# GpSimd fills a scratch tile behind each of its indirect transfers, from item 4 of the expert stage on as well

## The chip, the cores and the metric

The kernel runs on one core of a Trainium2 chip. The metric is the device time of one execution in microseconds (us); the time of a kernel is the median of its timed runs.

## The reference

Channel attention over four batches, and then a two-level mixture of experts over all 14592 tokens (four groups of four experts, so 16 experts; each token goes to one). Everything is float32.

```python
# attention: q, k, v are (4, 3648, 256)
qn = q / (np.linalg.norm(q, axis=1, keepdims=True) + 1e-06)
kn = k / (np.linalg.norm(k, axis=1, keepdims=True) + 1e-06)
a = softmax(kn.transpose(0, 2, 1) @ qn / tau)      # 256 x 256 for each batch
x = (v @ a).reshape(14592, 256)
# experts: one group g, then one expert e of that group for each token
h = np.maximum(x[tokens] @ w1[g, e], 0.0)          # w1[g, e]: 256 x 1024
out[tokens] = (g_w * e_w)[:, None] * (h @ w2[g, e])  # w2[g, e]: 1024 x 256
```

## The kernel before

The first third of the run is attention: it makes the rows x of all tokens and the expert of each token, and GpSimd writes each row by an indirect transfer (a scatter, line 444) into a DRAM array `x_sorted`, in which every expert has slots of its own. Behind each scatter GpSimd runs `pause()` (line 158), a memset of 128x256 float32 in the tile `zero`. That tile is read once, by the indirect transfer of `zero_rows` (line 561), which lies in the stage of items 0 to 3.

The rest is the expert stage. It works through 28 items of 512 tokens of one expert. For each item there are eight steps (f = 0 to 7) of 128 hidden columns: `ffn1` makes `hmm` in PSUM (line 899), ScalarE makes its rounded part `hh` (line 908) and VectorE the remainder `hl` (line 909), and two steps later `ffn2` adds `hh` and `hl` times the second weights into `wacc` (lines 919 and 920). When an item is done, `finish` scales its four tiles of 128 tokens into `ys` (lines 936 and 937), and `send` writes each by an indirect transfer of GpSimd to `out` (line 948). Items 0 to 3 read their rows from `x_sorted` by ordinary transfers of the SP queue; for items 4 to 27 `fetch_x` gathers them by one indirect transfer of GpSimd into `xg` (line 510, in `gather`), two items ahead. SP then copies `xg` in 16 pieces into `xq` (line 687, in `quads_of`), and VectorE turns `xq` into `xT` (line 735, in `turn_x`).

Beside items 4 to 27 run six quads: a quad holds 32 tokens each of four experts, worked on side by side. Their rows come by `q_rows` (a gather, line 510 too), their results go out by `q_put` (line 1042). A last part, for what is left in blocks of 128 tokens (`s_rows`, `s_put`), runs only as often as the data needs; its lines do not occur in this trace, apart from the memsets that set up its tiles.

GpSimd and SP run their instructions in the order in which the program writes them, in the expert stage the other engines too. In item i, GpSimd's order is: the four sends of item i-1 (behind step f = 1), the gather of item i+2 and, in every fourth item, the gather of the next quad (f = 3), and `q_put` (f = 3 of a quad's fourth item). SP's order is: half of the quad weights (f = 3), the first weights of item i+2 (f = 5, line 662), the other half (f = 6), the 16 pieces of item i+2 (f = 7), and then the second weights of the next item (f = 1). ScalarE and VectorE split the weights `wraw` into `ww` (lines 709 and 710). In step f = 4 of the last item GpSimd drains its queue and all engines read the number of remaining blocks (lines 1200 and 1201).

Before the change `pause()` stands behind every scatter, behind the gathers of items 4 and 5 (`if i < 2`: i counts from item 4 there) and behind the sends of items 0 to 3 (`KPRE` is 4). It does not stand behind the later gathers and sends, nor behind `q_rows` and `q_put`.

Of the kernel before, what the change touches and what calls it, by code (L numbers as in the profile page):

```python
# [37 lines left out]
KPRE = 4  # L38
# [22 lines left out]
def attention_moe(ctx: ExitStack, tc, q, k, v, tau, w_group, w_expert, w1, w2, out):  # L61
# [21 lines left out]
    def ring(*shape, name):  # L83
        return rp.tile([P, *shape], F32, tag="ring", name=name, bufs=RING)
# [71 lines left out]
    def pause():  # L156

        POOL.memset(zero[:, 0:256], 0.0)
# [349 lines left out]
    def gather(rows, ix, per):  # L508
        src = xs_d.rearrange("(n t) w -> n (t w)", t=per)
        POOL.indirect_dma_start(out=rows.bitcast(I32), out_offset=None, in_=src,  # L510
                                in_offset=bass.IndirectOffsetOnAxis(ap=ix, axis=0),
                                bounds_check=NSLOT // per - 1, oob_is_err=False)
# [138 lines left out]
    def raw_tile():  # L651
        return wp.tile([P, 2048], F32, tag="wraw", name="wraw", bufs=3)
# [11 lines left out]
    def fetch_x(d, tb, i):  # L664

        if d is items[0]:
            d["xg"] = raw_tile()[:, 0:4 * RW].rearrange("p (t w) -> p t w", t=4)
        else:
            d["xg"] = ring(4, RW, name="xg")
        d["nv"] = tb[1][:, i:i + 1]  # L670
        if tb is not tb_pre:
            gather(d["xg"].rearrange("p t w -> p (t w)"), tb[2][:, i:i + 1], 4)
            if i < 2:
                pause()
            return
        s = SP.value_load(tb[0][0:1, i, 1:2], min_val=0, max_val=DUMMY)
        ins = SP.dma_start(d["xg"].bitcast(I32), xs_d[ds(s, BIG), :].rearrange("(p t) w -> p t w", t=4))
        early.append(ins.ins)
        for o in late:
            tc.declare_no_dep(ins.ins, o, reason="the first items' slots have been filled")  # L680
# [78 lines left out]
    items = [dict() for _ in range(NBIG)]  # L759
# [73 lines left out]
    xsp = lambda i: (lambda: split_x(items[i]))  # L833
    fw = lambda i, which: (lambda: fetch_w(*where(i), which))
    fx = lambda i: (lambda: fetch_x(*where(i)))

    def where(i):
# [16 lines left out]
    for t in range(TM, len(xs_at)):  # L854
# [18 lines left out]
        if k == 8:  # L873
            fetch_w(items[0], tb_pre, 0, "w1")
            fetch_x(items[0], tb_pre, 0)
            fetch_w(items[0], tb_pre, 0, "w2")
# [3 lines left out]
        if x == UX - 1:  # L880
            fetch_x(items[1], tb_pre, 1)
            fetch_w(items[1], tb_pre, 1, "w1")
            split_x(items[0])
# [47 lines left out]
    def put(d, t, src, on):  # L931
        ys = d["ys"]
        wcol = d["wc"][:, t:t + 1]
        if len(d["acc"]) == 4:
            a = d["acc"][t]
            ACT.activation(ys[:, t, :], a[:, 1, :], AF.Copy, scale=wcol)
            DVE.scalar_tensor_tensor(ys[:, t, :], a[:, 0, :], wcol, ys[:, t, :], ALU.mult, ALU.add)  # L937
        elif on == 0:
            ACT.activation(ys[:, t, :], src, AF.Copy, scale=wcol)
        else:  # L940
            DVE.tensor_scalar(ys[:, t, :], src, wcol, None, ALU.mult)
        if any(d is o for o in items[0:2]):
            held.append((d, t))
        else:
            send(d, t)

    def send(d, t):
        ins = POOL.indirect_dma_start(  # L948
            out=out, out_offset=bass.IndirectOffsetOnAxis(ap=d["ids"][:, t:t + 1], axis=0),
            in_=d["ys"][:, t, :], in_offset=None, bounds_check=N - 1, oob_is_err=False)  # L950
        for o in yscat:
            tc.declare_no_dep(ins.ins, o, reason="every token is in one slot")
        yscat.append(ins.ins)
        if any(d is o for o in items[0:KPRE]):
            pause()

    held = []

    def send_late(i):
        return lambda: [send(d, t) for d, t in held if d is items[i]]  # L960
# [24 lines left out]

    def q_rows(q):
        gather(qs["xg"][q % 2], tb_pc[2][:, q:q + 1], 1)

    def q_weights(q, st, half):

        t = raw_tile() if half == 0 else None
        for k in range(2):
            p = 2 * half + k
            e = SP.value_load(tb_pc[0][0:1, 4 * q + p, 0:1], min_val=0, max_val=E - 1)
            w = t[:, k * 1024:(k + 1) * 1024] if half == 0 else rp.tile([P, 1024], F32, tag="L", name="qw", bufs=2)
            if st < 2:
                SP.dma_start(w.rearrange("p (c f) -> p c f", c=2),
                             w1e[ds(e, 1), :, st * 512:(st + 1) * 512].rearrange("o (c p) f -> p (o c) f", p=P))
            else:
                SP.dma_start(w.rearrange("p (c f) -> p c f", c=4),  # L1000
                             w2e[ds(e, 1), (st - 2) * 512:(st - 1) * 512, :].rearrange("o (c p) f -> p (o c) f", p=P))
            qs["w", p] = w
# [36 lines left out]
    def q_put(q):  # L1039
        ids = qs["ids"][q % 2]  # L1040
        DVE.tensor_scalar(qs["y"], qs["a"][:, 0:C], qs["xg"][q % 2][:, C + 1:C + 2], None, ALU.mult)
        ins = POOL.indirect_dma_start(
            out=out, out_offset=bass.IndirectOffsetOnAxis(ap=ids, axis=0),
            in_=qs["y"], in_offset=None, bounds_check=N - 1, oob_is_err=False)
        for o in yscat:
            tc.declare_no_dep(ins.ins, o, reason="every token is in one slot")
        yscat.append(ins.ins)


    raws, pb = {}, {}  # L1050
# [123 lines left out]
    for n in range(len(seq) + lag):  # L1174
# [3 lines left out]
        if n < len(seq):  # L1178
            i, f = seq[n]
            j, jn = host(i), host(i + 1)  # L1180
            if f == 3:
                if KPRE < i + 2 < NBIG:
                    fetch_x(*where(i + 2))
                if jn is not None:
                    if jn % 4 == 0:
                        q_rows(jn // 4)
                    q_weights(jn // 4, jn % 4, 0)
# [37 lines left out]
        if lag <= n < len(seq):  # L1225
            i, f = seq[n - lag]
# [4 lines left out]
        if n == len(seq) + lag - 1:  # L1231

            d = items[NBIG - 1]
            d["ys"] = ring(4, C, name="ys")
            for t in (0, 2, 1, 3):
                tsl, a, wcol = slice(t * P, (t + 1) * P), d["acc"][t], d["wc"][:, t:t + 1]
                for f in range(8 - TAIL, 8):
                    PE.matmul(a, d["h", f][0][:, tsl], d["w2w"][:, :, f, :], start=False, stop=(f == 7), skip_group_check=True)
                ACT.activation(d["ys"][:, t, :], a[:, 1, :], AF.Copy, scale=wcol)
                for f in range(8 - TAIL, 8):  # L1240
                    PE.matmul(a[:, 0, :], d["h", f][1][:, tsl], d["w2h"][:, f, :], start=False, stop=(f == 7), skip_group_check=True)
                DVE.scalar_tensor_tensor(d["ys"][:, t, :], a[:, 0, :], wcol, d["ys"][:, t, :], ALU.mult, ALU.add)
                send(d, t)
# [93 lines left out]
```

## Time and profile before

| | us |
|---|---|
| median of 3 runs (lowest to highest) | 950.46 (949.25 to 953.48) |
| the profiled execution, its own time | 950.95 |
| its span, first to last instruction | 949.1 |
| TensorE busy, matmuls | 923.4 |
| VectorE busy | 698.3 |
| ScalarE busy | 480.5 |
| GpSimd busy | 338.0 |

The profile is of one execution. PE is TensorE's matmuls, PEld its weight loads, DVE VectorE, ACT ScalarE, POOL GpSimd, SPq the queue of SP. In a list of instructions a row gives the start and the length in us, the engine, the line, the operation, the tile written and the tiles read, and in brackets how long the engine stood idle before it and what ended that. In a list of waits a row gives the waiting engine and line, what it waited for, the total, the number of times and the longest.

### The profile page before, as it was taken

How to read it: one execution, taken by the hardware profiler on the slowest of the kernel's cores; microseconds unless marked ns; L12 is line 12 of the kernel's file. 1: busy time of each engine (PE TensorE's matmuls, PEld its weight loads, DVE VectorE, ACT ScalarE, POOL GpSimd, SP SyncE). 2: the span in 40 equal slices, each digit the busy share in tenths (PEclk: the TensorE clock that was granted, in tenths of full speed). 3: DMA queues.
4: the chain of work that ended last, by engine and by line, in shares of the span. 5: the costliest groups of instructions: out<-in, count | busy, mean ns of one | idle time of the engine just before them, and what ended most of it. 6: DMA issues, size and time to landing. Idle time of an engine off the chain costs nothing.

```text
span 949.1 us, 16996 instructions
## 1 busy us (share of the span) xinstructions
PE 923.4 (97%) x5620; PEld 768.9 (81%) x5620; DVE 698.3 (74%) x1478; ACT 480.5 (51%) x791; POOL 338.0 (36%) x443
## 2 busy tenths in 40 slices
PE   8999999997999999999999999999999999999996
PEld 7899998987899988777877887877777887787784
DVE  6889888666889886867875687567775967577752
ACT  6787777565654544444444444444444444344431
POOL 0002998876588662222211222222222222222112
PEclk9999999999999999999999999999999999999999
DMA  9975868364755677677677767777776667766630
GB/s 305 356 262 200 308 225 280 113 227 156 252 178 178 189 260 241 218 235 244 221 230 227 251 243 241 242 251 245 244 242 225 237 221 233 224 232 219 216 118 27
DMA packets 159171, 213.96 MB, mean 225 GB/s; under 512 B 63107, under 2 KB 117643, under 8 KB 159072
## 3 DMA queue, kind: packets, MB, share of 16 engines
q1 hardware_dynamic: 144128, 168.23, 54.4%
q0 software_dynamic: 14944, 44.54, 12.5%
q8 instruction: 46, 0.75, 0.3%
q14 instruction: 53, 0.43, 0.2%
HBM read 170.33 MB, written 31.39 MB: 213 GB/s over the span
## 4 chain that ended last, share of the span: by engine, by line
PE 47%; issue 21%; DVE 10%; DMA 8%; POOL 4%; ACT 4%; SPq 3%; another core or an unknown queue 2%; POOLq 0%; DVEq 0%; ACTq 0%
PE hmm L899 16%; PE xmm L332 8%; PE wacc L919 7%; PE yacc L928 5%; PE wacc L920 4%; PE sacc L227 3%; DMA wraw<-in_moe_w 3%; DVE qhT L1007 2%; DMA qkraw<-in_k 2%; DMA qw<-in_moe_w 2%; POOL out L948 2%; PE vtr L312 2%; DVE ww L710 2%; DVE hl L909 1%
## 5 line engine op out<-in xcount | busy, mean ns | idle before, releaser
L899 PE MATMUL hmm<-xth,ww 128*128 128x512 f32 x896 | 316.6, 394 | 1.6 <-issue 1.5
L908 ACT ACTIVATE hh<-hmm 128x512 fp32r<-128x512 f32 x222 | 131.1, 598 | 311.6 <-PE hmm L899 249.4
L919 PE MATMUL wacc<-ww,hh 128*128 128x512 f32 x752 | 275.9, 398 | 0.4 <-issue 0.4
L909 DVE SCALAR_TENSOR_TENSOR hl<-hmm,hh 128x512 fp32r<-128x512 f32 x222 | 150.7, 686 | 161.4 <-ACT hh L908 151.5
L948 POOL DMA_INDIRECT out<-ys,ids x112 | 111.0, 991 | 436.9 <-DVE ys L937 394.8
L920 PE MATMUL wacc<-ww,hl 128*128 128x256 f32 x752 | 213.6, 284 | 2.7 <-issue 1.3
L899 PEld LDWEIGHTS hmm<-xth,ww 128*128 128x128 f32 x896 | 168.0, 188 | 39.8 <-issue 1.7
L899 PE MATMUL hmm<-xtl,ww 128*128 128x512 f32 x448 | 177.4, 396 | 0.2 <-DVE xtl L750 0.2
L919 PEld LDWEIGHTS wacc<-ww,hh 128*128 128x128 f32 x752 | 141.3, 188 | 41.6 <-issue 5.8
L444 POOL DMA_INDIRECT x_sorted<-xs,si x112 | 134.5, 1201 | 67.6 <-issue 34.6
L920 PEld LDWEIGHTS wacc<-ww,hl 128*128 128x128 f32 x752 | 141.1, 188 | 20.0 <-DVE hl L909 10.7
L710 DVE TENSOR_TENSOR ww<-wraw,ww 128x1024 fp32r<-128x1024 f32 x112 | 136.4, 1218 | 6.8 <-ACT ww L709 5.3
L709 ACT ACTIVATE ww<-wraw 128x1024 fp32r<-128x1024 f32 x112 | 118.3, 1057 | 0.0
L899 PEld LDWEIGHTS hmm<-xtl,ww 128*128 128x128 f32 x448 | 84.4, 188 | 11.8 <-issue 1.2
L227 PE MATMUL sacc<-qkraw 128*128 128x256 f32 (+1 forms) x360 | 86.9, 384 | 1.0 <-DMA qkraw<-in_k 1.0
L332 PE MATMUL xmm<-ahi,vth 128*128 128x276 f32 (+1 forms) x232 | 70.0, 304 | 6.5 <-issue 4.0
L227 PEld LDWEIGHTS sacc<-qkraw 128*128 128x128 f32 (+1 forms) x360 | 65.3, 192 | 9.8 <-issue 1.5
L332 PE MATMUL xmm<-alo,vth 128*128 128x276 f32 (+1 forms) x232 | 67.5, 292 | 0.4 <-DVE alo L292 0.4
L332 PE MATMUL xmm<-ahi,vtl 128*128 128x276 f32 (+1 forms) x232 | 66.9, 289 | 0.0
L211 DVE TENSOR_TENSOR sqa<-sqa,sq 128x2048 f32<-128x2048 f32 (+1 forms) x28 | 57.5, 2055 | 9.6 <-ACT sq L203 8.1
L335 ACT ACTIVATE xs<-xmm 128x276 f32<-128x276 f32 x112 | 43.4, 404 | 38.7 <-PE xmm L332 25.1
L1007 DVE STREAM_TRANSPOSE qhT<-qh 32x128 f32<-32x128 f32 x192 | 57.6, 300 | 2.7
(269 smaller groups left out, 1269.5 us busy)
## 6 DMA issues: line engine op xcount, KB each, us to landing
wraw<-in_moe_w SPq DMA_DIRECT2D x55, 1024.0 KB
wraw<-in_moe_w SPq DMA_DIRECT2D x50, 512.0 KB
qw<-in_moe_w SPq DMA_DIRECT2D x48, 512.0 KB
vr<-in_v SPq DMA_DIRECT2D x28, 512.0 KB
qkraw<-in_q SPq DMA_DIRECT2D x26, 512.0 KB
qkraw<-in_k SPq DMA_DIRECT2D x26, 512.0 KB
xq<-xg SPq DMA_DIRECT2D x368, 32.0 KB
x_sorted<-xs,si POOLq DMA_INDIRECT x112
```

What stands on the lines that cost most here:

```text
L227: PE.matmul(d["acc"][:, c, :], kt[:rows, 1, cs], qt[:rows, 0, :], start=d.pop("first", True) and c == 0, stop=(g == NG), skip_group_check= ...
L332: PE.matmul(mm[:rows, :NE], vt[:, c, j * P:j * P + rows], at[:, c, :], start=(n == 0), stop=(n == 5))
L444: ins = POOL.indirect_dma_start(out=xs_d, out_offset=bass.IndirectOffsetOnAxis(ap=si[:rows, j:j + 1], axis=0), in_=xs[:rows, t, 0:RW].bitc ...
L709: ACT.activation(whs[n][:, s], raw[:, s], AF.Copy)
L710: DVE.tensor_tensor(wls[n][:, s], raw[:, s], whs[n][:, s], ALU.subtract)
L899: PE.matmul(mm, wt[:, c, fs], xt[:, c, :], start=(n == 0), stop=(n == 5))
L908: ACT.activation(hh, mm, AF.Relu)
L909: d["hl"] = DVE.scalar_tensor_tensor(hl, mm, 0.0, hh, ALU.max, ALU.subtract)
L919: PE.matmul(d["acc"][t], hh[:, tsl], d["w2w"][:, :, f, :], start=(f == 0), stop=(f == 7), skip_group_check=True)
L920: PE.matmul(d["acc"][t][:, 0, :], hl[:, tsl], d["w2h"][:, f, :], start=False, stop=(f == 7), skip_group_check=True)
L948: ins = POOL.indirect_dma_start(out=out, out_offset=bass.IndirectOffsetOnAxis(ap=d["ids"][:, t:t + 1], axis=0), in_=d["ys"][:, t, :], in_o ...
L1007: DVE.transpose(dst[a * PC:(a + 1) * PC, :, p * PC:(p + 1) * PC], src[p * PC:(p + 1) * PC])
```

## The change

Three conditions fall away or are added: `pause()` now follows the gather of every item from 4 on, every send, every quad gather and every quad write. The gathers and writes of the remaining blocks (`s_rows`, `s_put`) get none.

```diff
@@ fetch_x
             gather(d["xg"].rearrange("p t w -> p (t w)"), tb[2][:, i:i + 1], 4)
-            if i < 2:
-                pause()
+            pause()
             return
@@ send
         yscat.append(ins.ins)
-        if any(d is o for o in items[0:KPRE]):
-            pause()
+        pause()
@@ q_rows
     def q_rows(q):
         gather(qs["xg"][q % 2], tb_pc[2][:, q:q + 1], 1)
+        pause()
@@ q_put
         yscat.append(ins.ins)
+        pause()
```

`pause` itself is unchanged:

```python
    def pause():
        POOL.memset(zero[:, 0:256], 0.0)
```

## Rows read from the trace of the kernel before

**Rows 1.** The page's first part: busy us, share of the span, instructions of each engine
```profile
PE 923.4 (97%) x5620; PEld 768.9 (81%) x5620; DVE 698.3 (74%) x1478; ACT 480.5 (51%) x791; POOL 338.0 (36%) x443
```

**Rows 2.** Waits of PE from 352 us on, all of them: total, times, longest
```profile
PE wacc L1241 <- ACT ys L1239: 2.3, 4, 0.6
PE hmm L899 <- issue: 1.5, 4, 0.6
PE wacc L920 <- issue: 1.3, 3, 0.8
PE wacc L919 <- issue: 0.4, 1, 0.4
PE wacc L920 <- DVE hl L909: 0.2, 1, 0.2
```

**Rows 3.** Waits of the weight loads (PEld) from 352 us on, two of them
```profile
PEld wacc L920 <- DVE hl L909: 10.7, 24, 0.7
...
PEld qacc L1035 <- DMA xq<-xg: 0.7, 2, 0.4
```

**Rows 4.** Groups of POOL's instructions: busy us, mean ns, idle before
```profile
L158 POOL MEMSET zero<- 128x256 f32 x134 | 44.7, 334 | 0.1
```

**Rows 5.** POOL's instructions in order of time where sends are paused
```profile
347.46 0.33 POOL L158 MEMSET zero<- 128x256 f32 x1
347.95 0.97 POOL L948 DMA_INDIRECT out<-ys,ids  x1 [0.16 <-issue]
348.92 0.33 POOL L158 MEMSET zero<- 128x256 f32 x1
349.42 0.97 POOL L948 DMA_INDIRECT out<-ys,ids  x1 [0.16 <-issue]
```

**Rows 6.** POOL's instructions in order of time in a later item, without pauses
```profile
645.78 1.00 POOL L948 DMA_INDIRECT out<-ys,ids  x1 [13.21 <-DVE ys L937]
647.08 0.97 POOL L948 DMA_INDIRECT out<-ys,ids  x1 [0.30 <-issue]
...
650.92 1.05 POOL L510 DMA_INDIRECT xg<-x_sorted,ix_big  x1 [0.30 <-issue]
```

**Rows 7.** Waits of SP's queue between 400 and 900 us, the longest
```profile
SPq L687 <- DMA xg<-x_sorted,ix_big: 40.0, 16, 5.8
```

**Rows 8.** SP's queue in order of time, the same item
```profile
657.97 11.83 SPq L687 DMA_DIRECT2D xq<-xg  x16
670.65 0.41 SPq L662 DMA_DIRECT2D wraw<-in_moe_w  x1
674.26 2.17 SPq L1000 DMA_DIRECT2D wraw<-in_moe_w  x2
```

**Rows 9.** ACT's instructions in order of time, the first use of the weights fetched at 670.65
```profile
681.95 1.05 ACT L709 ACTIVATE ww<-wraw 128x1024 fp32r<-128x1024 f32 x1
683.68 0.60 ACT L908 ACTIVATE hh<-hmm 128x512 fp32r<-128x512 f32 x1 [0.68 <-PE hmm L899]
```

**Rows 10.** DVE's instructions in order of time, the turn of the pieces copied from 657.97 on
```profile
679.24 1.23 DVE L735 STREAM_TRANSPOSE xT<-xq 128x1024 f32<-128x1024 f32 x1
```

**Rows 11.** DVE's instructions in order of time beside the pauses of rows 5
```profile
347.34 0.69 DVE L909 SCALAR_TENSOR_TENSOR hl<-hmm,hh 128x512 fp32r<-128x512 f32 x1 [0.72 <-ACT ys L939]
348.29 1.23 DVE L710 TENSOR_TENSOR ww<-wraw,ww 128x1024 fp32r<-128x1024 f32 x1 [0.26 <-issue]
```

**Rows 12.** DVE's instructions in order of time beside the unpaused sends of rows 6
```profile
646.59 0.68 DVE L909 SCALAR_TENSOR_TENSOR hl<-hmm,hh 128x512 fp32r<-128x512 f32 x1
647.19 1.21 DVE L710 TENSOR_TENSOR ww<-wraw,ww 128x1024 fp32r<-128x1024 f32 x1
```

**Rows 13.** A small DVE operation: its group between 400 and 900 us, and one early instruction
```profile
L523 DVE TENSOR_SCALAR ids<-ids 128x4 int32<-128x4 int32 x20 | 3.4, 170 | 0.7
...
290.57 0.44 DVE L523 TENSOR_SCALAR ids<-ids 128x4 int32<-128x4 int32 x1
```

**Rows 14.** POOL's instruction beside that early one
```profile
290.34 0.98 POOL L444 DMA_INDIRECT x_sorted<-xs,si  x1 [0.17 <-issue]
```

**Rows 15.** POOL's last instructions in order of time
```profile
926.15 0.97 POOL L1042 DMA_INDIRECT out<-qy,qid  x1 [3.04 <-DVE qy L1041]
...
943.83 0.97 POOL L948 DMA_INDIRECT out<-ys,ids  x1 [1.26 <-DVE ys L1242]
```

## Prediction

> **What bounds the kernel now.** I read the busy shares first: TensorE's matmuls are busy for 97% of the span, GpSimd for 36% [rows 1]. A busy share is an average, so I read next, for the part that the change touches (from 352 us, when the last existing pause is over, to the end), who TensorE waited for. The whole list comes to 5.7 us (2.3 + 1.5 + 1.3 + 0.4 + 0.2) in 597 us [rows 2], and 2.3 of it is the tail, where the last four tiles wait for ScalarE. No line of it names GpSimd or a transfer. So in this stretch the kernel runs at the pace of its matmuls, and work added to GpSimd reaches the end only if it makes something late that TensorE needs. Three things could be that, so I looked at each: VectorE's `hl`, for which the weight loads wait once per item, 24 times and 10.7 us [rows 3]; the rows and weights that SP fetches behind a gather; and the very last write.
>
> **How many, and how long.** The change adds a memset behind 22 gathers (items 6 to 27), 96 sends (24 items by 4), 6 quad gathers and 6 quad writes: 130. One takes 334 ns as the profile reports it [rows 4], so 130 x 0.334 = 43.4 us of GpSimd time. GpSimd has room: before the first send of an item it had stood idle for 13.21 us [rows 6]. So what counts is only how much later the transfers behind a pause start. Where sends are paused, one starts 349.42 - 347.95 = 1.47 us after the other [rows 5]. Without pauses, four sends and the gather behind them are (650.92 - 645.78) / 4 = 1.285 us apart [rows 6]. A pause thus pushes the next transfer back by 0.185 us, because most of it fits into the 0.30 us that lay between two transfers anyway. The gather behind four sends starts 4 x 0.185 = 0.74 us later, a quad gather behind it 0.93. The first send is not moved: it waits for `ys` [rows 6].
>
> The Trainium skill, "Perfetto Trace Analysis", section "GPSIMD Engine Instruction", says to time such instructions by the spacing of their starts and not by their reported span. The rows bear it out: 0.334 reported, 0.185 in spacing. By the reported span the gather would be 4 x 0.334 = 1.34 us late.
>
> **What waits behind the gather.** SP is queued behind it: its 16 pieces wait for the gathered rows, 40.0 us in 16 waits [rows 7], and the next item's second weights stand behind them. In the item I followed, the gather is issued by 650.92 + 1.05 = 651.97, and the pieces start at 657.97 [rows 6, 8], so up to 6.0 us pass from issue to landing. A gather that is 0.74 later moves the pieces and the weight fetch at 670.65 by 0.74. The next fetch, at 674.26 [rows 8], starts 3.2 us after the end of that one, so SP catches up inside the item and nothing adds up from item to item.
>
> Who needs them? The pieces are all issued at 657.97 + 11.83 = 669.80, and VectorE turns them at 679.24 without having waited [rows 8, 10]: 9.4 us. Their landing time has no row; bounded from above by the gather's 6.0 us (544 KB against 32 KB each), 3.4 us of cover are left. The weights fetched at 670.65 are first used at 681.95 by ScalarE [rows 8, 9], with no idle time ahead of it: 11.3 us of cover less a landing that no row gives. If that cover were gone, ScalarE would start 0.74 late, and its next instruction had 0.68 us of idle time ahead of it [rows 9], so that about 0.1 us would be left. I take 0; the ends are 0 and 24 x 0.1 = 2.4 us, and no gain, since a later gather makes nothing earlier.
>
> **VectorE beside a memset.** The first pause of an item begins where the first send ends, at about 645.78 + 1.00 = 646.78, inside the `hl` of 646.59 to 647.27 [rows 6, 12]. That `hl` is the one that the weight loads wait for, so its growth reaches TensorE undiminished. The nearest rows are exact pairs: with a whole pause inside it (347.46 to 347.79) the same instruction took 0.69, without one 0.68 [rows 5, 11, 12]; the weight split took 1.23 with a pause inside and 1.21 without. I take 24 x 0.01 = 0.24 us; the ends are 0 and 24 x 0.03 = 0.7 us, if both growths fell on the path.
>
> **The tail.** The four last sends wait 1.26 us each for VectorE [rows 15], more than a pause of 0.33. The pause behind the last one runs while that send lands: the send is issued by 943.83 + 0.97 = 944.80 and the span ends at 949.1, 4.3 us later. I take 0; the ends are 0 and 0.33. The drain in the last item stands behind the last quad write, which ends at 927.12 [rows 15]; the next send could be issued only some 10 us later, so a pause ahead of the drain is covered.
>
> **Sum.** The profiled execution took 950.95 us, 949.1 of it span. Added: 0.24 + 0 + 0 = 0.2, so 951.2. The median of the runs shown is 0.5 below the profiled execution, which puts the forecast at 950.7. The bounds add up to -0 and +3.4 us (2.4 + 0.7 + 0.33); the runs shown spread from 949.25 to 953.48.
>
> **Rivals.**
> First, the lock, the one that ends slower. GpSimd and VectorE could exclude each other for a whole instruction. The trace shows that this happens: a small VectorE operation took 0.44 us at 290.57, against 0.17 on the mean, while GpSimd wrote descriptors from 290.34 to 291.32 [rows 13, 14]. If the memset did that to the late `hl`, each of 24 items would lose up to 0.334 us: 8.0 us, 958.5. It decides as soon as that `hl` grows by more than 0.2 us (24 x 0.2 = 4.8 us, 0.5%). Against it: `hl` with a pause inside it at 347.34 took 0.69 [rows 11]. The Trainium skill, "SBUF — State Buffer", section "Who interferes with whom", states such an exclusive lock, but only against VectorE's two-port modes, and against operations with two SBUF inputs only where GpSimd reads SBUF; a memset only writes, and the rows of `hl` and of the weight split agree.
>
> Second, the gather chain, slower too. If the pieces or weights had no cover and ScalarE's idle time did not take it up, each of 22 gathers would hand on 0.74 us: 16.3 us, 966.8. Against it: 9.4 and 11.3 us of distance, and no transfer in TensorE's waits.
>
> Third, faster: pauses spread GpSimd's transfers, and SP's loads could land earlier in between. For it speaks that SP waits 40 us for gathers. Against it: the only transfer for which the weight loads waited is 0.7 us in total [rows 3], and all of TensorE's waits outside the tail are 3.4 us [rows 2]. It gives at best 950.5 - 3.4 = 947.1, less than 0.5%. Over 0.5% faster would need matmuls themselves to get faster, which no row suggests.
>
> Fourth, that the change does not do what it says, the new memsets being absent or standing elsewhere: 950.5.
>
> **How the numbers follow.** Forecast 0.86, the lock 0.05, the gather chain 0.03, spread transfers 0.03, no effect of the edit 0.03. Within 0.5% (4.75 us, about what a measurement of this kernel can tell from no change) lie the forecast, the fourth rival and a third of the third rival: 0.90. Slower by over 0.5%: 0.08, the lock and the gather chain. Faster by over 0.5%: 0.02, the rest of the third. The range takes the forecast with the sum's bounds and the spread of the runs: down to 948.5 (0.75 below the lowest run, for a little of the third rival), up to 954.2 (950.7 + 3.4). The first two rivals stay outside.
>
> **What would show it.** In the profile of the changed kernel: 264 memsets of line 158 instead of 134; sends of an item 1.47 us apart; the gather 0.74 us later behind its first send; SP's waits for `xg` longer by some 16 x 0.7 = 11 us in total, and nothing of it in TensorE's waits; `hl` at 0.69 at most beside a pause; an unchanged tail. I am wrong if `hl` grows by a third of a microsecond there, if ScalarE's weight split begins to wait for a transfer, or if TensorE's list of waits grows beyond some 10 us.

## The result and the profile after

The changed kernel took 936.4 us in the median of 4 runs (934.84 to 941.22), the kernel before 951.17 in the 4 runs beside them (949.25 to 953.48). The ratio is 0.9851 with a 95% interval of [0.9816, 0.9885]: 1.5% faster, where I had forecast no change. The profiled execution took 935.83 us, 934.1 of it span.

The page's first part for the kernel after (busy us, share of the span, instructions; answers [rows 1]), and the group of its memsets (busy us, mean ns, idle before; answers [rows 4]):

```profile
PE 916.0 (98%) x5620; PEld 771.7 (83%) x5620; DVE 707.0 (76%) x1478; ACT 481.4 (52%) x791; POOL 403.1 (43%) x573
...
L158 POOL MEMSET zero<- 128x256 f32 x264 | 87.8, 333 | 0.3
```

GpSimd has its 130 memsets more, and works 65 us longer, in a kernel that is 15 us shorter. **Where is the time gone?** The first send of an item is a good mark on the clock. These are the first sends of items 5 and 27, first in the kernel before, then in the kernel after (GpSimd's instructions in order of time):

```profile
370.27 1.00 POOL L948 DMA_INDIRECT out<-ys,ids  x1 [16.89 <-DVE ys L937]
...
918.30 0.97 POOL L948 DMA_INDIRECT out<-ys,ids  x1 [18.90 <-DVE ys L937]
```

```profile
367.57 1.01 POOL L947 DMA_INDIRECT out<-ys,ids  x1 [16.26 <-DVE ys L936]
...
903.25 0.97 POOL L947 DMA_INDIRECT out<-ys,ids  x1 [16.10 <-DVE ys L936]
```

I call the time between them the stretch: 22 items, 918.30 - 370.27 = 548.03 us before and 903.25 - 367.57 = 535.68 after. So 12.35 of the 15.0 us came in the stretch. The other 2.70 (370.27 - 367.57) were there before the first changed instruction had run: the first send of all starts at 321.38 before and at 318.67 after. The change can't have made those; its own share in the two profiled executions is 12.35 us, 1.3%. Behind the stretch nothing moved (949.1 - 918.30 = 30.8, 934.1 - 903.25 = 30.85).

The busy times of the engines in the stretch, before and then after (length, then for PE, PEld, DVE, ACT and POOL the busy us and the number of instructions; then granted clock, DMA share, GB/s):

```profile
370.27:918.30 548.03, 543.46 (x3158) 429.82 (x3148) 391.29 (x769) 242.88 (x384) 118.78 (x120) 1.00 0.70 231
```

```profile
367.57:903.25 535.68, 535.68 (x3158) 431.88 (x3148) 400.69 (x769) 244.45 (x384) 179.73 (x238) 1.00 0.72 237
```

After the change TensorE's matmuls fill the stretch without a gap. Of the 12.35 us, 548.03 - 543.46 = 4.57 had been idle time. The other 7.78 had stood inside the busy figure, at the same granted clock: the records of two neighbouring matmuls overlap, so a short standstill between them does not show as idle. An example comes below.

**Who stopped waiting?** The waits of the weight loads from 352 us on in the kernel after (total, times, longest), which answer [rows 3], and then the whole list of PE's waits, which answers [rows 2]:

```profile
PEld wacc L918 <- issue: 7.4, 18, 0.4
...
PEld wacc L918 <- DVE hl L908: 0.4, 1, 0.4
```

```profile
PE wacc L1241 <- ACT ys L1239: 2.3, 4, 0.6
```

(The lines shown from 673 to `q_put` count one less in the kernel after: its L908 is the L909 of before.) The row of 10.7 us in which the weight loads of line 920 waited for VectorE's `hl` [rows 3] is gone; the 0.4 that is left is a wait of the line before it, and stood in the list of before too. Of PE's 5.7 us only the tail's 2.3 are left. These two drops, 10.7 and 3.4, can't be added up to a gain: what a load waits is not what the matmuls lose. The loss itself is the distance between the starts of neighbouring matmuls, in the trace of before, over the median distance of the same pair in the trace of after. Summed up so, some 6 us of the 12.35 lay ahead of matmuls that read `hl`, and the rest ahead of those that read `hh` or make `hmm`, for which the lists mostly name nobody ("issue"). About half was lost 6 to 10 us behind an item's first send, the other half 15 to 22 us behind it. So the gain is the end of TensorE's standstills, and of the producers that the lists name for them `hl` has by far the most.

**Why was `hl` late?** `hl` needs ScalarE's `hh`, and that needs TensorE's `hmm`. What ScalarE waited for between 400 and 900 us, the longest rows, before and then after:

```profile
ACT hh L908 <- PE hmm L899: 176.8, 95, 8.1
ACT hh L908 <- remote: 42.5, 6, 7.9
```

```profile
ACT hh L907 <- PE hmm L898: 247.0, 140, 3.2
```

A wait of ScalarE for the next matmul is nothing to worry about as such. But in the kernel before single ones last up to 8.1 us, and some end on something that the profile can't name ("remote"). An example from the kernel before: TensorE, ScalarE and VectorE beside one train of sends, which here means the four sends of an item, one behind the other (first send at 670.63), and then a weight load and four matmuls. `qmm` is a quad's product, and `qh` what ScalarE makes of it.

```profile
671.77 0.39 PE L1022 MATMUL qmm<-qw,qxT 128*32 128x256 f32 x2
...
674.77 0.39 PE L899 MATMUL hmm<-xth,ww 128*128 128x512 f32 x1
```

```profile
675.04 0.60 ACT L1026 ACTIVATE qh<-qmm 128x512 f32<-128x512 f32 x1 [3.17 <-remote]
678.00 1.09 ACT L908 ACTIVATE hh<-hmm 128x512 fp32r<-128x512 f32 x2 [2.36 <-PE hmm L899]
```

```profile
678.63 0.69 DVE L909 SCALAR_TENSOR_TENSOR hl<-hmm,hh 128x512 fp32r<-128x512 f32 x1 [5.37 <-ACT hh L908]
...
691.56 1.89 DVE L909 SCALAR_TENSOR_TENSOR hl<-hmm,hh 128x512 fp32r<-128x512 f32 x3
```

```profile
692.30 0.19 PEld L920 LDWEIGHTS wacc<-ww,hl 128*128 128x128 f32 x1 [0.52 <-DVE hl L909]
```

```profile
691.82 0.40 PE L919 MATMUL wacc<-ww,hh 128*128 128x512 f32 x1
692.30 0.39 PE L920 MATMUL wacc<-ww,hl 128*128 128x256 f32 x1
692.53 0.39 PE L919 MATMUL wacc<-ww,hh 128*128 128x512 f32 x1
692.76 0.28 PE L920 MATMUL wacc<-ww,hl 128*128 128x256 f32 x1
```

The quad's last matmul ends at 671.77 + 0.39 = 672.16, and ScalarE, which stands idle, starts on its result at 675.04, 2.9 us later. The last matmul of the fourth step ends at 675.16, and `hh` starts at 678.00, 2.8 later, in one go with the `hh` of the next step. In the trace's own record of TensorE's semaphore that step's update stands at 677.98. TensorE itself goes on at its pace meanwhile; it is the message "done" that comes late. VectorE, idle for 5.37 us, then works off what has piled up without a gap to speak of, and some 14 us later weight loads stand for an `hl`. There the matmul with `hl` starts 0.48 us behind its neighbour instead of 0.23 (692.76 - 692.53): 0.25 us are lost, the weight load had stood for 0.52, and between the two matmul records lie only 0.08 us (692.30 - 692.22). This is how a loss hides in a busy share. In 20 of the 22 items of the stretch the `hh` of the fourth step starts 1.8 to 4.9 us after its matmuls; in one it is 1.1 us, in one 0.04. In the kernel after it is 0.04 us in all 22:

```profile
661.32 0.39 PE L1021 MATMUL qmm<-qw,qxT 128*32 128x256 f32 x2
...
664.32 0.39 PE L898 MATMUL hmm<-xth,ww 128*128 128x512 f32 x1
```

```profile
663.02 0.60 ACT L1025 ACTIVATE qh<-qmm 128x512 f32<-128x512 f32 x1 [1.50 <-PE qmm L1021]
664.74 0.60 ACT L907 ACTIVATE hh<-hmm 128x512 fp32r<-128x512 f32 x1 [1.12 <-PE hmm L898]
```

The fourth step's matmuls end at 664.71 and `hh` starts at 664.74; the quad's result waits 1.3 us (663.02 - 661.71) instead of 2.9.

**What did the pauses do to the sends?** GpSimd and VectorE in the kernel after, in the same item (answers [rows 6] and [rows 12]):

```profile
660.57 1.01 POOL L947 DMA_INDIRECT out<-ys,ids  x1 [16.07 <-DVE ys L936]
661.58 0.33 POOL L158 MEMSET zero<- 128x256 f32 x1
662.08 1.98 POOL L947 DMA_INDIRECT out<-ys,ids  x1 [0.17 <-DVE hl L908]
...
664.55 0.98 POOL L947 DMA_INDIRECT out<-ys,ids  x1 [0.16 <-issue]
...
666.02 0.98 POOL L947 DMA_INDIRECT out<-ys,ids  x1 [0.16 <-issue]
...
667.48 1.06 POOL L510 DMA_INDIRECT xg<-x_sorted,ix_big  x1 [0.16 <-issue]
```

```profile
661.38 0.68 DVE L908 SCALAR_TENSOR_TENSOR hl<-hmm,hh 128x512 fp32r<-128x512 f32 x1
661.98 1.22 DVE L709 TENSOR_TENSOR ww<-wraw,ww 128x1024 fp32r<-128x1024 f32 x1
```

The sends start 0, 1.51, 3.98 and 5.45 us after the first; without pauses it was 1.30 from one to the next [rows 6]. The large step is not the pause's. The second send takes 1.98 us where the others take 0.98 to 1.01, and it starts 0.10 us after VectorE's weight split (661.98): the split keeps its 1.22 us, the send ends late. Before, the second send stood ahead of the split (647.08 against 647.19 [rows 6, 12]) and took 0.97.

Two things had thus changed at once: small pauses, and one large gap between two sends. And one item of the kernel before makes the sends suspect. Its third send comes late, for a reason that the trace does not name:

```profile
746.02 1.00 POOL L948 DMA_INDIRECT out<-ys,ids  x1 [12.96 <-DVE ys L937]
747.32 0.98 POOL L948 DMA_INDIRECT out<-ys,ids  x1 [0.30 <-issue]
749.81 0.97 POOL L948 DMA_INDIRECT out<-ys,ids  x1 [1.51 <-issue]
```

```profile
746.33 0.60 ACT L1026 ACTIVATE qh<-qmm 128x512 f32<-128x512 f32 x1 [0.31 <-PE qmm L1022]
749.24 0.60 ACT L908 ACTIVATE hh<-hmm 128x512 fp32r<-128x512 f32 x1 [2.31 <-PE hmm L899]
```

There the quad's result is taken at once, and the `hh` of the fourth step is 0.04 us late, in the only one of the 22 items, with no pause at all.

### The profile page after: what moved, and what is told of

It is laid out like the page before. It is cut to its first block, busy times and chain, and to the rows that moved or that the text cites. A ratio compares the mean times of both kernels' runs of the same rounds, so it can differ in the third digit from the quotient of the medians.

```text
span 934.1 us, 17126 instructions
## 1 busy us (share of the span) xinstructions
PE 916.0 (98%) x5620; PEld 771.7 (83%) x5620; DVE 707.0 (76%) x1478; ACT 481.4 (52%) x791; POOL 403.1 (43%) x573
## 4 chain that ended last, share of the span: by engine, by line
PE 73%; issue 9%; DMA 5%; POOL 5%; DVE 4%; ACT 3%; SPq 1%; POOLq 0%; ACTq 0%; DVEq 0%
PE hmm L898 28%; PE wacc L918 16%; PE wacc L919 8%; PE xmm L332 6%; PE yacc L927 5%; PE sacc L227 4%; DMA qkraw<-in_k 3%; POOL out L947 2%; PE qacc L1034 2%; PE qmm L1021 2%; PE vtr L312 2%; DVE sqa L211 2%; POOL x_sorted L444 1%; POOL zero L158 1%; DMA xg<-x_sorted,ix_big 1%
## 5 line engine op out<-in xcount | busy, mean ns | idle before, releaser
L907 ACT ACTIVATE hh<-hmm 128x512 fp32r<-128x512 f32 x222 | 133.6, 602 | 346.7 <-PE hmm L898 316.1
L947 POOL DMA_INDIRECT out<-ys,ids x112 | 133.8, 1195 | 385.0 <-DVE ys L936 355.4
L908 DVE SCALAR_TENSOR_TENSOR hl<-hmm,hh 128x512 fp32r<-128x512 f32 x222 | 153.0, 690 | 133.8 <-ACT hh L907 118.9
L919 PE MATMUL wacc<-ww,hl 128*128 128x256 f32 x752 | 210.8, 280 | 0.0
L158 POOL MEMSET zero<- 128x256 f32 x264 | 87.8, 333 | 0.3
```

The costliest lines, as they stand in the source:

```text
L907: ACT.activation(hh, mm, AF.Relu)
L908: d["hl"] = DVE.scalar_tensor_tensor(hl, mm, 0.0, hh, ALU.max, ALU.subtract)
L919: PE.matmul(d["acc"][t][:, 0, :], hl[:, tsl], d["w2h"][:, f, :], start=False, stop=(f == 7), skip_group_check=True)
L947: ins = POOL.indirect_dma_start(out=out, out_offset=bass.IndirectOffsetOnAxis(ap=d["ids"][:, t:t + 1], axis=0), in_=d["ys"][:, t, :], in_o ...
```

## The experiments

They ran on three chips, the kernel before beside them each time; whether the chip of the result is one of them is not on record. The kernel before took 941.1 us on the first, 928.1 on the second, 941.6 and 943.4 on the third (two groups of runs). Every time is compared with the runs of before on the same chip. No trace of the kernel before was kept there, so where a trace is said to look like before, the trace above is meant. "Stretch" is worked out from the first sends of items 5 and 27 as above, "late" is the start of `hh` behind the end of its matmuls in the fourth step.

The theories by their letters: G, the pauses leave gaps between the sends in which TensorE's completions get through, the more the longer the gap. O, the other pauses (behind gathers and quads) bring the gain. P, what counts is that the second send no longer starts ahead of VectorE's weight split. And for the last group: S, the gap between two sends is what counts, whatever makes it; T, the meeting of send and split is needed.

### First group: which pauses

Pauses behind the sends alone:

```diff
-        if any(d is o for o in items[0:KPRE]):
-            pause()
+        pause()          # in send; gathers, q_rows and q_put as before
```

> The new pauses stand only behind the sends of items 4 to 27; those behind the gathers, the quad gathers and the quad writes are taken back. Theory G (gaps): a matmul's completion reaches ScalarE late while indirect transfers follow each other 1.285 us apart, and a pause between two transfers lets it through; nearly all pauses between two transfers are those behind sends, so 935 to 939. Theory P (phase): it matters only where the second send starts against VectorE's split of the weights (0.1 us ahead of it before, 0.1 us behind it after); the pause behind the first send is there, so 935 to 939 too. Theory O (the other pauses, those behind the gathers and quad transfers, bring the gain): 949 to 952.

934.23 us, ratio 0.9924 [0.9894, 0.9954]; stretch 535.68, `hh` in time. The pauses behind the sends alone give the stretch of the changed kernel, to the hundredth. (The us expected in this group were meant for a kernel before of 951. As a ratio, 935 to 939 is 0.983 to 0.987, which this run misses. In its profile 7.6 us pass from the start of the last send to the end, against 5.3 in the kernels before and after; why isn't shown.)

All other pauses, and none behind the sends:

```diff
             gather(d["xg"].rearrange("p t w -> p (t w)"), tb[2][:, i:i + 1], 4)
-            if i < 2:
-                pause()
+            pause()          # likewise in q_rows and q_put; send as before
```

> The new pauses stand only behind the gathers of items 6 to 27, the quad gathers and the quad writes; the sends of items 4 to 27 have none. Theories G and P: the four sends of an item stay 1.285 us apart and the second starts ahead of the weight split, so no gain: 948 to 952. Theory O: 935 to 939.

942.64 us, 1.0012 [0.9991, 1.0032]; stretch 550.43. The weight loads still wait for `hl`:

```profile
PEld wacc L919 <- DVE hl L908: 9.5, 22, 0.5
```

The pauses behind gathers and quads bring nothing.

One pause per item, behind its first send:

```diff
-        if any(d is o for o in items[0:KPRE]):
+        if any(d is o for o in items[0:KPRE]) or t == 0:
             pause()
```

> One new pause for each item only, behind its first send (t == 0). Theory P: the second send falls behind the start of the weight split and takes near 2 us, as in the changed kernel; nearly the whole gain, 935 to 940. Theory G: one gap of four is widened, and the other three transfers still follow each other at 1.285 us: a quarter to a half of the gain, 943 to 949. In the profile theory P wants ScalarE to start hh on time in every item.

930.99 us, 0.9881 [0.9859, 0.9903]; stretch 535.68. One memset of 0.33 us in an item gives the stretch that the 130 give. The second send starts 1.5 us behind the first and takes 1.98.

The other three pauses, without that one:

```diff
-        if any(d is o for o in items[0:KPRE]):
+        if any(d is o for o in items[0:KPRE]) or t > 0:
             pause()
```

> New pauses behind the second, third and fourth send of each item, none behind the first. Theory P: the second send keeps its place ahead of the weight split, so no gain, 948 to 952. Theory G: three of four gaps are widened, so half to three quarters of the gain or more, 936 to 943.

937.0 us, 0.9959 [0.9942, 0.9977]; stretch 541.24. Here the sends stand 1.48 us apart from the second on, and the `hh` is late by 1.0 us or more in 18 of the 22 items. Three pauses give less than half of what one gives, and the ratio lies between the ranges of the two theories (as ratios 0.984 to 0.991 for G, 0.997 to 1.001 for P). That speaks against a gain in proportion to the gaps, and for something about the place of the second send. So the next runs set G against P.

### Second group: G against P, on a chip that doesn't show the effect

Shorter memsets behind the first send, so that the second starts just ahead of or just behind the split:

```diff
-    def pause():
-        POOL.memset(zero[:, 0:256], 0.0)
+    def pause(w=256):
+        POOL.memset(zero[:, 0:w], 0.0)
...
         if any(d is o for o in items[0:KPRE]):
             pause()
+        elif t == 0:
+            pause(128)       # 192 in the second kernel
```

> As the run with one pause behind the first send of each item, but that memset fills 128 columns instead of 256, some 0.2 us, so that the second send starts only some 0.07 us later than before: at 1.38 us behind the first, still ahead of the weight split at 1.41. Theory P (the second send must not start ahead of the split): no gain, a ratio of 0.998 to 1.002. Theory G (each widened gap helps by its width): a third of the gain, a ratio of about 0.996.

> The same with 192 columns, some 0.27 us: the second send starts some 0.14 us later than before, at 1.44 us behind the first, just behind the start of the split at 1.41. Theory P: the whole gain, a ratio of 0.986 to 0.991, and a second send that takes near 2 us. Theory G: two thirds of the gain, 0.992.

No new pause, the split one step earlier:

```diff
-                if f in (1, 2):
-                    split_w(i + 1, "w1", f - 1)
+                if f in (0, 1):
+                    split_w(i + 1, "w1", f)
```

> No new pause at all. Instead the two splits of an item's first weights stand one step earlier (steps 0 and 1 instead of 1 and 2), so that no split begins while the second send is issued. Theory P: hh of step 3 comes on time and the gain is there without any pause, a ratio of 0.985 to 0.992. Theory G: the sends follow each other as closely as before, hh of step 3 stays late, 0.998 to 1.004. It could also lose something of its own, if the earlier split waits for its weights; then ScalarE's split shows a wait for a transfer.

And the changed kernel again:

> The changed kernel itself on the same chip, for comparison with the others of this group. All theories: the same ratio as the run with pauses behind all sends, 0.987 to 0.993.

928.18, 927.99, 929.13 and 928.17 us, ratios 1.0002 [0.9992, 1.0012], 1.0002 [0.9993, 1.0012], 1.001 [1.0, 1.002] and 1.000 [0.999, 1.001]. Nothing can be told apart, because here the kernel before, at 928.13, is as fast as all of them, and every profiled kernel has a stretch of 535.67 to 535.69. The kernel with the split one step earlier has its sends 1.31 us apart there, as in the kernel before, and its `hh` 0.04 us late in all items. The changed kernel, for which 0.987 to 0.993 had been expected, gains nothing. So on this chip the completions are in time although the sends stand close. The same kernels were then run on the third chip, with the one pause of 256 columns beside them.

### Third group: the same on a chip that shows it

> One pause per item, behind its first send. Anchor for the three kernels beside it. On a chip on which the kernel before takes about 940 us or more, G and P both expect 0.985 to 0.990 of the time of the kernel before, the second send at 1.51 us behind the first, no wait of the weight loads for hl (under 1 us in total), and every hh of the fourth step within 0.1 us of its matmuls. On a chip on which the kernel before takes about 928 us, both expect 1.000 and nothing can be told apart.

929.4 us, 0.9891 [0.9867, 0.9914]; stretch 535.68, `hh` late by 0.04 in all 22 items. The gain is there again.

> The memset behind the first send writes 128 columns, not 256, so that the second send comes about 0.1 us later than before, at 1.40 us, and still not later than the start of VectorE's weight split at 1.41. G (the gap counts, in proportion): nearly half of the gain of the full pause, 0.993 to 0.996. P (the second send must start behind VectorE's split): nothing, 0.999 to 1.001, with 7 to 11 us of weight-load waits for hl as before. Only on a chip on which the kernel before takes about 940 us or more; else 1.000 under both.

940.13 us, 0.9981 [0.9965, 0.9997]; stretch 546.50, `hh` late by 1.0 us or more in 20 of 22 items.

> The memset behind the first send writes 192 columns, so that the second send could start at about 1.45 us, just behind the start of VectorE's split at 1.41. G: three quarters of the gain of the full pause, 0.990 to 0.993. P: the second send takes about 2 us because VectorE's split holds it, and the whole gain comes, 0.985 to 0.990; if it still slips ahead of the split, nothing. Only on a chip on which the kernel before takes about 940 us or more.

929.09 us, 0.9878 [0.986, 0.9895]; stretch 535.68, `hh` in time. GpSimd in one item of the kernel with 128 columns, and VectorE's split there:

```profile
660.65 0.23 POOL L158 MEMSET zero<- 128x128 f32 x1
661.06 0.99 POOL L948 DMA_INDIRECT out<-ys,ids  x1 [0.17 <-issue]
662.35 0.98 POOL L948 DMA_INDIRECT out<-ys,ids  x1 [0.30 <-issue]
```

```profile
661.06 1.25 DVE L710 TENSOR_TENSOR ww<-wraw,ww 128x1024 fp32r<-128x1024 f32 x1
```

The same with 192 columns:

```profile
655.18 0.28 POOL L158 MEMSET zero<- 128x192 f32 x1
655.63 2.04 POOL L948 DMA_INDIRECT out<-ys,ids  x1 [0.17 <-issue]
657.97 0.98 POOL L948 DMA_INDIRECT out<-ys,ids  x1 [0.30 <-DMA xq<-xg]
```

```profile
655.58 1.22 DVE L710 TENSOR_TENSOR ww<-wraw,ww 128x1024 fp32r<-128x1024 f32 x1
```

A memset that is 0.05 us longer decides over the whole gain. With 128 columns send and split start together, the send takes 0.99 us and the next follows 1.29 us after it. With 192 the split is 0.05 us ahead, the send takes 2.04, and the next follows 2.34 us after it. G's proportion (nearly half, three quarters) is refuted: 0.9981 [0.9965, 0.9997] and 0.9878 [0.986, 0.9895] lie outside its ranges. What P says of the second send holds so far.

The Trainium skill, "SBUF — State Buffer", section "Who interferes with whom", says that a VectorE instruction with two SBUF inputs contends with a GpSimd instruction that reads SBUF, and that the order of issue decides who is blocked. `ww<-wraw,ww` has two SBUF inputs, and a send takes its list `ids` from SBUF. The rows agree for one order: with the split ahead the send is held (2.04 instead of 0.98) and the split keeps its 1.22. For the other order they show no such block: in the kernel before the send starts 0.11 us ahead, and the split behind it keeps its 1.21 [rows 6, 12]. The same section also tells of a probe in which an operation of this kind (`tensor_tensor`) did not stall transfers that GpSimd issues; here it did. That the hold is this lock is the page's word; the runs show the hold.

> No new pause at all; the two halves of the next item's weight split are called one step earlier (f 0 and 1 in place of 1 and 2), so that VectorE's split ends before the first send starts and the sends keep the spacing of the kernel before, 1.29 us. G: the sends are as close as before, so the late completions stay: 0.998 to 1.002. P as first stated (the second send must not stand ahead of the split): the order is no longer as in the kernel before, and if the meeting of send and split is what makes the completions late, they come in time: 0.985 to 0.990; if it is the hold that helps, by opening a gap of 2 us between the second and third send, nothing changes: 0.998 to 1.002. Only on a chip on which the kernel before takes about 940 us or more.

950.46 us, 1.0088 [1.006, 1.0115]: slower than before, and outside every range expected. Send and split don't meet, no send is held, the sends stand 1.29 us apart, and late completions are there: in 16 of the 22 items the `hh` of the fourth step is late by 1.0 us or more. In five others with sends as close it is in time. There the fourth step's matmuls end 2.97 us behind the first send and not 4.1, and the `hh` of the fifth step is late instead, by 0.6 to 1.5 us. So it also matters when a step ends against the sends. In the profiled execution, the longest of the five (960.14 us), the stretch is 559.43, and TensorE itself now stands for the quad's `qh`:

```profile
PE hmm L899 <- ACT qh L1026: 10.7, 5, 2.5
```

This execution already reached its first send at 318.89 us, against 312.49 with 128 columns, before anything changed, so not all of its length is the edit's. To take send and split apart is not the cure. Either the hold itself helps, or the gap that it opens ahead of the third send.

The kernels with 128 columns show in passing what differs between the chips. The same kernel, what ScalarE waited for between 400 and 900 us, first on the second chip (928.18 us), then on the third (940.13):

```profile
ACT hh L908 <- PE hmm L899: 263.7, 142, 3.2
```

```profile
ACT hh L908 <- PE hmm L899: 175.0, 90, 6.2
ACT hh L908 <- remote: 41.0, 6, 7.9
```

On the second chip no wait of ScalarE is longer than 3.2 us and none ends on "remote"; on the third it looks like the kernel before, and the weight loads of line 920 wait 10.2 us for `hl`.

### Fourth group: the gap without the hold

Four memsets in a row make the gap, on the same third chip. Behind the second send, with the split one step earlier, so that it meets no send:

```diff
         if any(d is o for o in items[0:KPRE]):
             pause()
+        elif t == 1:
+            for _ in range(4):
+                pause()
...
-                if f in (1, 2):
-                    split_w(i + 1, "w1", f - 1)
+                if f in (0, 1):
+                    split_w(i + 1, "w1", f)
```

> VectorE's split one step earlier, so that it meets no send, as in the kernel that took 1.009 of the time of before; and four memsets behind the second send of an item, so that the third comes about 2.5 us behind the second, where the hold had put it. S (the distance between second and third send is what brings the gain, whatever makes it): hh of the fourth step in time again, and 0.985 to 0.992 on a chip on which the kernel before takes about 940 us or more. T (the meeting itself is needed, the hold of a send by VectorE's split): 1.005 to 1.010, the late hh stay. On a chip with 928 us before, 1.000 under both.

932.17 us, 0.9896 [0.9868, 0.9924]; stretch 535.67, `hh` late by 0.04 in all items. GpSimd in one of them:

```profile
655.18 0.98 POOL L948 DMA_INDIRECT out<-ys,ids  x1 [0.30 <-issue]
656.14 1.46 POOL L158 MEMSET zero<- 128x256 f32 x4
658.10 0.98 POOL L948 DMA_INDIRECT out<-ys,ids  x1 [0.50 <-issue]
```

No send is held (0.98), the gap is 2.92 us, and the stretch has the whole gain.

The same memsets with the split in its old place (the first half of that diff alone):

> Only the four memsets behind the second send; split and second send stay where they are, so the second send stands ahead of the split at 1.31 us and runs unheld, and the third comes at about 3.8 us. S: 0.985 to 0.992, hh in time. T: 0.995 to 1.001, hh of the fourth step late by 2.5 to 4.9 us as before. On a chip with 928 us before, 1.000 under both.

932.72 us, 0.9901 [0.9864, 0.9937]; stretch 535.68. Again without a hold.

The same memsets one send later (`elif t == 2`):

> The same four memsets, but behind the third send, so that three sends stand 1.3 us apart as before and the fourth follows some 2.5 us later. S in its narrow form (the gap must come behind the second send, ahead of the third): most of the late hh stay, 0.995 to 1.001. S in its wide form (any gap of 2.5 us within the train does it): 0.985 to 0.992. T: 0.995 to 1.001.

932.56 us, 0.9895 [0.987, 0.992]; stretch 535.68. The first three sends stand 1.3 us apart as before, and `hh` starts at most 0.9 us late, which reaches nobody. Of the two places tested, behind the second send and behind the third, the place hardly counts.

The changed kernel beside them:

> The changed kernel beside these three. On a chip on which the kernel before takes about 940 us or more: 0.985 to 0.993 under all theories, its second send held by the split for 1.98 us. It gives the gain against which the others are read. On a chip with 928 us before: 1.000.

930.26 us, 0.9875 [0.9848, 0.9902]; stretch 535.68. The three kernels with four memsets lie 2 us above this one. In their profiles 7.0 to 7.5 us pass from the start of the last send to the end, here 5.0; the pauses behind the sends alone had 7.6 without four memsets, so why is open.

**Together**, the largest step between neighbouring sends of an item (of most items, each from the profile) against the stretch:

| kernel | largest step, us | stretch, us | ratio |
|---|---|---|---|
| split earlier | 1.31 | 559.43 | 1.0088 |
| 128 columns | 1.40 | 546.50 | 0.9981 |
| pauses behind the later sends | 1.48 | 541.24 | 0.9959 |
| one pause (256 columns, send held) | 2.29 | 535.68 | 0.9891 |
| 192 columns (send held) | 2.34 | 535.68 | 0.9878 |
| the change (send held) | 2.47 | 535.68 | 0.9875 |
| four memsets, not held | 2.9 | 535.67 to 535.68 | 0.9895 to 0.9901 |

(The third row is from the first chip, the others from the third.) Where the gain came, there is a gap of about 2.3 us or more somewhere in the train of four sends. The single late send at 746 us in the kernel before says the same. The theory of the meeting (T) falls: the two kernels with four memsets behind the second send have no hold and the whole gain. Between 1.5 and 2.2 us no kernel was run, so where the edge lies is open. And one rival stands untested: every kernel with the gain also starts its fourth send later, 5.1 to 5.5 us behind the first in most items, the others 3.9 to 4.3. Whether it takes one wide gap, or the same delay spread evenly would do, no run tells apart.

**What stays open.** Why TensorE's completions come late while GpSimd's transfers follow each other at 1.3 us, why a gap ends that, and why it doesn't happen on the second chip, no run here shows. Each chip was measured at one time only (the third twice within minutes), so what is lasting in a chip and what was its state at the time aren't told apart. That the spacing of the sends decides is shown by the edits that move nothing but the sends and the transfers behind them; in which way it does, isn't.

## Why the prediction was wrong

**What held.** 264 memsets of 333 ns; 87.8 - 44.7 = 43.1 us of GpSimd time where I worked out 43.4. The `hl` with a pause inside it took 0.68 us, so VectorE beside a memset costs nothing (I took 0.24 us in all). From the third send on the spacing is 1.47. The tail is as before: GpSimd's last send waits 0.33 less, because the pause lies there, and 5.3 us pass from its start to the end of the span as before (934.1 - 928.77 and 949.1 - 943.83 [rows 15]):

```profile
928.77 0.97 POOL L947 DMA_INDIRECT out<-ys,ids  x1 [0.93 <-DVE ys L1242]
```

**The gather: size wrong, conclusion right.** It starts 667.48 - 660.57 = 6.91 us behind the first send instead of 5.14 [rows 6], 1.77 later and not 0.74, because of the held send, and SP's waits for it grew by 39.8 us (from 40.0 [rows 7]), not by 11:

```profile
SPq L686 <- DMA xg<-x_sorted,ix_big: 79.8, 20, 5.9
```

Nothing of that reached TensorE: its lists after the change name no transfer. So the cover of 9.4 and 11.3 us was enough for 1.77, and the second rival (the gather chain) was rightly small.

**The lock: seen, but at the wrong instruction.** I weighed it for the memset beside `hl`, where it doesn't act. My row for it proved little: behind the 0.44 us at 290.57 VectorE's next instruction starts already at 290.74, 0.17 us later, the operation's mean length [rows 13], so that row shows no hold. And the `hl` at 646.59 is not the one that the weight loads wait for: their waits for `hl` come 10 to 22 us behind an item's first send, this `hl` 0.8 us behind it. My own numbers had the other meeting in them: with pauses the second send starts 1.47 us behind the first, so at 645.78 + 1.47 = 647.25 [rows 6], and VectorE's split starts at 647.19 [rows 12]. Without pauses the send was ahead, with them it is behind by 0.06. The change moved an instruction past another, and I had asked only what the memset meets, not what the moved sends meet. That alone wouldn't have turned the sign: a held send looks like a cost.

**The step that failed is the bound of the third rival.** I gave the spread transfers at best 3.4 us, with two reasons. The first took the matmuls' own waits [rows 2] as the ceiling of any gain. It left out the 10.7 us of the weight loads for `hl` [rows 3], which stood in the next group and which I treated as something that could only grow. And it took a list of idle times for the loss, when 7.78 of the 12.35 us stood inside the busy figure. (3.4 and 10.7 make 14.1, near the 12.35 that came, but that is partly luck: in the example 0.52 us of a load's wait cost the matmuls 0.25, and waits that name nobody fell away too.) The second reason was that no wait of TensorE names a transfer. That is true, and still true; a list names only the last link. I never followed it back: `hl` waited for `hh` and `hh` for a completion that the profile calls "remote" or puts down to a matmul that had long ended. The path was not the rival's either: SP's loads did not land earlier, its waits for `xg` doubled, and TensorE still gained. What the runs showed in its place is that spreading the sends lets TensorE's completions reach ScalarE in time, which was worth 12.35 us. I also wrote that the loads wait for `hl` once per item. In the 22 items of the stretch they do it in 12, up to three times in one, and in the others not at all, and this unevenness asks for a cause outside the regular work. "Over 0.5% faster would need matmuls themselves to get faster" was the wrong conclusion from a busy share of 97%: the same matmuls did come out shorter in busy time, because their standstills had been counted in it.

Two slips moved nothing: 950.7 + 3.4 is 954.1 and not 954.2, and of the four last sends the first waits 10.0 us for VectorE, only the other three 1.26.

**Could it have been seen?** In part. The trace of before holds the item at 746 us, with a gap between two sends and everything in time, beside 20 items with neither. That would have supported a case for faster with a price: some 10 us if the pauses make such a gap. Whether pauses of 0.185 us do so depends on 0.05 to 0.1 us at the split, which rows 6 and 12 leave just decidable. A chance of 0.02 for faster was far too low for what the profile showed. On a chip like the second one my forecast of no change would have come true, but not for my reasons: it would have been luck.

## What to carry to other kernels

When you bound what a change can bring, don't take idle time for the whole loss, since overlapping records hide standstills in the busy share: look at the distance between the starts of its instructions. Look at the waits of every queue of the bounding engine, weight loads too, and for each ask what makes its producer late, link by link, until you reach work or something that the profile can't name; then look in the trace for an item in which the suspect is absent. When a change delays instructions, list what the delayed ones now meet on other engines, not only what the new ones meet. A train of indirect transfers from GpSimd can be worth a deliberate gap even where no one waits for GpSimd, but measure on more than one chip: here one memset per item is worth 1.1 to 1.2% on two of them, and on another the whole change, and one memset of 192 columns per item, were worth nothing.

## What the hardware showed that I had not expected

- TensorE's message that a matmul is done reached ScalarE up to 4.9 us late in the fourth step beside four indirect transfers 1.3 us apart, while the matmuls ran on; with one gap of about 2.3 us or more in the train it reached it after 0.04 us in the changed kernel (0.9 at most in any kernel with such a gap).
- It was not the same on all chips: the kernel before took 951.2, 941.1 and 941.6 to 943.4 us where it occurred, 928.1 where it didn't. Part of these differences lies elsewhere, as the 2.70 us ahead of the changed instructions show.
- An indirect transfer of GpSimd that starts 0.05 us behind a VectorE operation with two SBUF inputs of 1.22 us takes 2.04 us instead of 0.98; if it starts with it, it takes 0.99 and VectorE 1.25; if it starts 0.11 us ahead, 0.97 and VectorE 1.21.
- TensorE's busy time fell by 7.78 us in the stretch with the same 3158 matmuls at the same granted clock: standstills between overlapping matmul records had been counted as busy.
